# A fixed order for the first four attention tiles of a chunked-attention and two-FFN kernel

## The chip, the cores and the metric

The kernel runs on one NeuronCore of a Trainium2 chip. The metric is the device time of one execution in microseconds (us), lower is better. TensorE is called PE here, its weight loads PEld, VectorE DVE, ScalarE ACT, GpSimd POOL, SyncE SP.

## What is computed

Attention over chunks, then two feed-forward layers, all in float32 at the outputs. The inputs `q`, `k`, `v` have 4 batches, 8 heads, 768 positions and 64 columns. A chunk of 32 queries sees 8 memory keys, 16 positions to the left, its own 32 and 8 to the right, so 64 keys in all:

```python
scores = scale * q_c @ concat(mem_k, k_ctx).T      # per chunk: 32 x 64
scores = scores - max(scores)
a = exp(scores); a = a / (sum(a) + 1e-9)
out_c = a @ concat(mem_v, v_ctx)                   # 32 x 64
x = heads side by side                             # 3072 x 512
h = x @ w_in;  x = (h - tanh(h)) @ w_out           # FFN 1, 512 -> 2048 -> 512
h = x @ w_in2; y = (max(h,0) + alpha*min(h,0)) @ w_out2   # FFN 2
```

The weights arrive as 64-bit floats.

## The kernel before

**Tiles.** 128 queries are one attention tile; there are 24. FFN 1 works in six blocks of four tiles, with 16 column groups `f` of 128 hidden columns in each: `emit_h` (12 matmuls), `emit_g` (tanh and the split of the result into a high and a low part), `emit_y` (12 matmuls). FFN 2 follows with a form that needs fewer products. Every float32 operand of the FFNs is kept as a high and a low part (`fp32r`), and three products of parts make one product.

**One attention tile** takes these steps. `emit_scores` (L516): PE writes the scores `sp` to two PSUM tiles of the pool `ps_a` (two buffers); DVE takes the row maximum and the maximum is subtracted (for the first three tiles ACT copies the scores to SBUF and POOL subtracts, afterwards DVE does both), ACT takes the exponential. `emit_soft` (L557): DVE sums the row and inverts the sum, POOL multiplies. Then the 32-row blocks of the result are transposed into `ebuf`, a buffer with zeros between the blocks. For the first four tiles (`PE_T`) `emit_turn` (L581) does this on PE: products with an identity `ident` write the blocks into the PSUM tile `tp` (`ps_y`), products with a tile `zeros` write the zero blocks (L589), and ACT copies the whole `tp` to `ebuf` (L601), in two halves of four heads. Later tiles use DVE's transpose. `emit_pv` (L603): PE multiplies by the values into `pv` (`ps_h`), ACT copies it to the high part of `ring` (L616) and DVE writes the low part (L617). Block 0 of FFN 1 reads the `ring` entries of all four first tiles.

**Weights.** `split_w` (L121) converts a pair of 64-bit weight tiles of one `f`: per tile one ACT pass (L99), three DVE passes (`u` L102, L105, `s` L109), then ACT makes the high part (L115) and POOL the low part (L116). `u` lies in `ps_y` while `stage["early"]` holds, in `ps_a` afterwards.

**Order.** SP's loads of the first phase are issued in the order written: keys and queries of tiles 0 and 1 with the values of tile 0, the weight pair of `f` = 0, then the rest (`loads_to`, `loads`). All other engines are ordered by a scheduler of the compiler, from the order in which the program emits the steps: tile after tile, with the conversions of `f` = 0, 1 and 2 (`EARLY_W`) emitted at tiles 1, 4 and 5, and the scores of tile 4 before the first FFN product. In block 0 a further `f` is converted in each slot (`more_w`), and the later tiles are worked off at planned slots between the FFN products.

Of the kernel before, what the change touches and what calls it, by code (L numbers as in the profile page):

```python
# [7 lines left out]
FP32 = mybir.dt.float32  # L8
FP32R = mybir.dt.float32r
# [13 lines left out]
FIRST = 1  # L23
EARLY_W = (1, 4, 5)
PE_T = 4
ANCHOR = 'exp'
SUB_POOL = 3
# [4 lines left out]
AHEAD = 5  # L32
# [4 lines left out]
def chunk_attention_two_ffn_kernel(  # L37
# [55 lines left out]

    def to_f32(raw, dst=None):
        words = raw.bitcast(U32).rearrange("p (n two) -> p n two", two=2)
        lw, hw = words[:, :, 0], words[:, :, 1]
        pool, tag = (ps_y, "y") if stage.get("early") else (ps_a, "a")
        u = pool.tile([128, 512], U32, tag=tag, name="u")
        nc.scalar.activation(  # L99
            out=u.bitcast(FP32), in_=hw.bitcast(FP32), func=ACTF.Copy, scale=2.0 ** -112  # L100
        )
        nc.vector.tensor_scalar(  # L102
            out=u, in0=u, scalar1=3, scalar2=None, op0=ALU.logical_shift_left
        )
# [7 lines left out]
        return s.bitcast(FP32)  # L112

    def split_f32(v, hi, lo):
# [371 lines left out]
    ident = ac.tile([128, 128], FP32, name="ident")  # L486
    zeros = ac.tile([128, CH], FP32, name="zeros")
    qt, vt, kt = {}, {}, {}
# [26 lines left out]

    def emit_scores(t):  # L516
        s = t % TPS
        kn = kt.pop(t)
        sps = [ps_a.tile([128, HP, 64], FP32, tag="a", name="sp",
                         padded_shape=[128, 8, 64]) for _ in range(2)]  # L520
        for p in range(HP):
            for c in range(4):
                for j in range(2):
                    r = slice(64 * j, 64 * j + 64)
                    last["at"] = nc.tensor.matmul(  # L525
                        out=sps[j][CH * c:CH * c + CH, p, :],
                        lhsT=qt[t][r, p, CH * c:CH * c + CH],
                        rhs=kn[r, p, c // 2, CH * (c % 2):CH * (c % 2) + W + NM],
                        start=True, stop=True,
                    ).ins  # L530
        for sp in sps:
            if s == 0:
# [14 lines left out]
        else:  # L547
            for j, sp in enumerate(sps):
# [4 lines left out]
                )  # L553
        last["exp"] = nc.scalar.activation(out=sc, in_=sc, func=ACTF.Exp, scale=scale).ins
        sm[t] = sc

    def emit_soft(t):  # L557
        sc = sm.pop(t)
        sg = aw.tile([128, H, 1], FP32, tag="sg", name="sg")
# [5 lines left out]
        )  # L565
        if t < PE_T:
            return emit_turn(sc)
        et = t_p.tile([128, 512], FP32, tag="t", name="et")
# [11 lines left out]

    def emit_turn(sc):  # L581
        idn = ident.rearrange("p (a c n) -> p a c n", a=2, c=2)
        for hh in range(2):
            tp = ps_y.tile([128, 512], FP32, tag="y", name="tp")
            tp = tp[:KW].rearrange("k (a h n) -> k a h n", a=2, h=4)
            for c in range(2):
                cols = slice(CH * c, CH * c + CH)
                r = 2 * CH * (1 - c)
                nc.tensor.matmul(  # L589
                    out=tp[r:r + CH, :, :, cols], lhsT=zeros, rhs=sc[:, 4 * hh:4 * hh + 4, :],  # L590
                    start=True, stop=True,
                )
                for h in range(4):
                    for a in range(2):
# [5 lines left out]
                        )  # L600
            nc.scalar.activation(out=ebuf[:, :, 4 * hh:4 * hh + 4, :], in_=tp, func=ACTF.Copy)  # L601

    def emit_pv(t, slot):  # L603
        pv = ps_h.tile([128, 512], FP32, tag="h", name="pv")
        for p in range(HP):
            for a in range(2):
                for j in range(2):
# [3 lines left out]
                        lhsT=vt[t][:, a, D * h:D * h + D],  # L611
                        rhs=ebuf[:, a, h, :],
                        start=True, stop=True,
                    ).ins
        pvv = pv.rearrange("k (p n) -> k p n", p=HP)
        nc.scalar.activation(out=ring[0][:, slot], in_=pvv, func=ACTF.Copy)  # L616
# [49 lines left out]
    if True:  # L666
# [15 lines left out]
        n0 = blocks1[0]  # L682
        nc.gpsimd.memset(zeros, 0.0)
        nc.gpsimd.memset(ident, 0.0)
# [211 lines left out]
```

## Time and profile before

| | us |
|---|---|
| median of 3 runs (lowest, highest) | 1112.61 (1108.74, 1112.82) |
| the profiled execution, its own time | 1111.79 |
| its span, first to last instruction | 1110.0 |
| PE busy | 1082.4 (98%) |
| DVE, ACT, POOL busy | 523.6, 478.4, 426.8 |

The span is what the hardware profiler saw from the first to the last instruction; 1.8 us of the execution's own time lie around it. Busy times are sums over the span and hide that the phases have different limits: the first 50 us are attention and weight loading, the rest is the FFNs with attention tiles between their products.

### The profile page before, as it was taken

What the parts mean: (1) busy time and instruction counts of PE and PEld (TensorE: products, weight loads), DVE (VectorE), ACT (ScalarE), POOL (GpSimd) and SP (SyncE); (2) the same over time, 40 slices, a digit from 0 to 9 for tenths busy, and PEclk for the clock granted to TensorE, in tenths of its full rate; (3) what the DMA queues carried; (4) which work ended last, traced back from release to release, by engine and by line L of the source; (5) the groups of instructions that cost most, each with busy time, mean ns of one, the idle gap of its engine ahead of it and who ended that gap; (6) DMA issues with size and microseconds to landing.
All of it is one profiled execution on the core that took longest, in us unless ns stands there. A gap on an engine that the chain in (4) does not pass through costs nothing.

```text
span 1110.0 us, 17747 instructions
## 1 busy us (share of the span) xinstructions
PE 1082.4 (98%) x7056; PEld 892.5 (80%) x7056; DVE 523.6 (47%) x875; ACT 478.4 (43%) x789; POOL 426.8 (38%) x279
## 2 busy tenths in 40 slices
PE   4699999999999999999999999999999999999998
PEld 4588888888888888888888888888888888888887
DVE  3688754655646565564311466700566500566000
ACT  3566643443534444443332466520556420557300
POOL 3266633443434343344462000990002990003900
PEclk9699999999999999999999999999999999999999
DMA  9673234554454455335420663543754443751312
GB/s 275 258 265 115 77 124 171 164 147 166 143 176 176 154 162 170 125 148 189 176 67 1 232 214 110 180 164 106 234 194 152 152 161 129 246 175 39 110 43 76
DMA packets 57395, 171.04 MB, mean 154 GB/s; under 512 B 8288, under 2 KB 8544, under 8 KB 57312
## 3 DMA queue, kind: packets, MB, share of 16 engines
q1 hardware_dynamic: 53712, 163.48, 44.1%
q10 hardware_dynamic: 3600, 6.42, 1.6%
q8 instruction: 56, 0.92, 0.3%
q14 instruction: 27, 0.22, 0.1%
HBM read 134.23 MB, written 35.65 MB: 153 GB/s over the span
## 4 chain that ended last, share of the span: by engine, by line
PE 96%; DMA 2%; DVE 1%; issue 1%; POOL 0%; ACT 0%; SPq 0%; ACTq 0%; DVEq 0%; POOLq 0%
PE h L241 24%; PE y L280 24%; PE h L368 20%; PE yb L445 12%; PE y L445 12%; PE pv L609 2%; PE sp L525 2%; PE tp L596 1%; DMA qn<-in_q_dram 1%; DMA ri<-in_moe_w_in_dram 1%; DMA y1d<-ys 0%; PE tp L589 0%; DVE u L102 0%; SPq L495 0%; DVE s L109 0%
## 5 line engine op out<-in xcount | busy, mean ns | idle before, releaser
L241 PE MATMUL h<-ring,wt 128*128 128x512 f32 x1152 | 281.2, 392 | 4.0 <-ACT ring L616 2.2
L241 PEld LDWEIGHTS h<-ring,wt 128*128 128x128 f32 x1152 | 216.9, 189 | 50.7 <-ACT ring L616 2.4
L116 POOL TENSOR_TENSOR g2l<-g,g2h 128x1024 fp32r<-128x1024 f32 x48 | 121.7, 2570 | 282.1 <-ACT g2h L115 282.1
L368 PE MATMUL h<-xh,wi 128*128 128x512 f32 x672 | 209.0, 389 | 0.2 <-DVE g L385 0.2
L280 PE MATMUL y<-gh,wt 128*128 128x512 f32 x768 | 192.7, 391 | 0.0
L266 POOL TENSOR_TENSOR gl<-t,gh 128x512 fp32r<-128x512 f32 x96 | 126.7, 1320 | 155.3 <-ACT gh L265 129.2
L280 PEld LDWEIGHTS y<-gh,wt 128*128 128x128 f32 x768 | 143.2, 188 | 30.4
L368 PEld LDWEIGHTS h<-xh,wi 128*128 128x128 f32 x672 | 126.1, 188 | 27.0 <-DVE g L385 0.6
L257 DVE TENSOR_TENSOR t<-h,t 128x512 f32<-128x512 f32 x96 | 65.7, 685 | 153.6 <-ACT t L256 148.8
L256 ACT ACTIVATE t<-h 128x512 f32<-128x512 f32 x96 | 57.0, 594 | 130.2 <-PE h L241 118.8
L280 PE MATMUL y<-gl,wt 128*128 128x512 f32 x384 | 104.2, 389 | 0.0
L469 DVE COPY ys<-y 128x512 f32<-128x512 f32 x6 | 4.0, 688 | 198.6 <-PE y L445 198.6
L445 PE MATMUL y<-ring,g2h 128*128 128x512 f32 x384 | 96.3, 389 | 0.0
L445 PE MATMUL yb<-ring,g2h 128*128 128x512 f32 x384 | 96.1, 389 | 0.0
L445 PEld LDWEIGHTS y<-ring,g2h 128*128 128x128 f32 x384 | 72.1, 188 | 15.0
L445 PEld LDWEIGHTS yb<-ring,g2h 128*128 128x128 f32 x384 | 72.1, 188 | 15.0
L280 PEld LDWEIGHTS y<-gl,wt 128*128 128x128 f32 x384 | 72.0, 188 | 15.0
L265 ACT ACTIVATE gh<-t 128x512 fp32r<-128x512 f32 x96 | 60.5, 630 | 42.7 <-DVE t L257 34.9
L376 ACT ACTIVATE n<-g 128x512 f32<-128x512 f32 x72 | 45.4, 632 | 72.6 <-DVE g L385 72.2
L368 PE MATMUL h<-xl,wi 128*128 128x512 f32 x192 | 74.7, 389 | 0.0
L378 DVE SCALAR_TENSOR_TENSOR g<-g,n 128x512 f32<-128x512 f32 x72 | 62.7, 870 | 15.8 <-ACT n L377 14.5
L377 ACT ACTIVATE n<-n,alpha_neg 128x512 f32<-128x512 f32 x96 | 67.0, 717 | 1.3
(86 smaller groups left out, 1313.2 us busy)
## 6 DMA issues: line engine op xcount, KB each, us to landing
wi<-w2i SPq DMA_DIRECT2D x72, 512.0 KB, 4.4
ring<-w2o SPq DMA_DIRECT2D x48, 512.0 KB, 3.6
kn<-in_k_dram SPq DMA_DIRECT2D x24, 384.0 KB, 5.1
vn<-in_v_dram SPq DMA_DIRECT2D x24, 384.0 KB, 4.1
ri<-in_moe_w_in_dram SPq DMA_DIRECT2D x16, 512.0 KB, 8.3
ro<-in_moe_w_out_dram SPq DMA_DIRECT2D x16, 512.0 KB, 8.6
pk<-in_moe_w_in_dram SPq DMA_DIRECT2D x16, 512.0 KB, 3.7
w2i<-ws SPq DMA_DIRECT2D x16, 512.0 KB, 2.7
```

The source lines that it names most:

```text
L116: nc.gpsimd.tensor_tensor(out=lo, in0=v, in1=f32(hi), op=ALU.subtract)
L241: last["ffn"] = nc.tensor.matmul(out=h, lhsT=wi[:, a, kk, :], rhs=ring[c][:, s0:s0 + n, kk, :], start=(i == 0), stop=(i == 3 * KD - 1),).ins
L256: nc.scalar.activation(out=t, in_=h, func=ACTF.Tanh)
L257: last["dve"] = nc.vector.tensor_tensor(out=t, in0=h, in1=t, op=ALU.subtract).ins
L265: nc.scalar.activation(out=gh, in_=t, func=ACTF.Copy)
L266: nc.gpsimd.tensor_tensor(out=gl, in0=t, in1=f32(gh), op=ALU.subtract)
L280: mm = nc.tensor.matmul(out=yp[l, b][j][:, :n * 128], lhsT=wo[:, a, j * 128:(j + 1) * 128], rhs=g[c], start=first, stop=final,)
L368: nc.tensor.matmul(out=h, lhsT=w[:, a, 128 * kt:128 * kt + 128], rhs=x[c][:, kt, :], start=(first and j == 0), stop=(j == 5), skip_group_c ...
L376: nc.scalar.activation(out=n, in_=h, func=ACTF.Relu, scale=-1.0)
L377: nc.scalar.activation(out=n, in_=n, func=ACTF.Copy, scale=alpha_neg[:, f:f + 1])
L378: nc.vector.scalar_tensor_tensor(out=t, in0=h, scalar=0.0, in1=n, op0=ALU.max, op1=ALU.add)
L445: nc.tensor.matmul(out=sets[k][j], lhsT=g[a][:, k, j * 128:(j + 1) * 128], rhs=w[:, c, :], start=(f == 0 and n == 0), stop=(f == NF - 1 an ...
```

## The change

- The first four tiles are emitted in steps in one written order (`FIRST_STEPS`), and PE, ACT, DVE and POOL keep that order in this phase. A letter is a step, a digit the tile (for a, b, c the weight tile of `f` = 0): S scores, M maximum and subtraction, E exponential, N sum and multiplication, T transposes and copies, P product with the values, R `ring`; a ACT's pass over both raw weight tiles, b DVE's three passes, c the split.
- The products with `zeros` are gone. Each of the first four tiles has its own buffer `eb` in the weight pool, zeroed by a POOL memset of 96 x 1024 elements (and `ebuf` likewise for the later tiles); from `tp` only the blocks are copied, per half two copies on ACT and one on DVE.
- The loads come in another order: the first weight pair stands behind keys and queries of all four tiles and two tiles of values.
- Only `f` = 0 is converted within the fixed order. The scores of tile 4, its softmax and the conversion of `f` = 1 and 2 are emitted after it. `u` always lies in `ps_a`.

```diff
-EARLY_W = (1, 4, 5)
-PE_T = 4
+FIRST_STEPS = """
+S0 M0 S1 E0 N0 M1 E1 T0 N1 S2 M2 P0 R0 S3 E2 M3 E3 T1 N2 N3 a0 P1 b0 R1 c0 T2 b1 c1 T3 P2 R2 P3 R3
+"""
+MANUAL = ("PE", "Activation", "DVE", "Pool")
...
     def emit_turn(...):
...
-                r = 2 * CH * (1 - c)
-                nc.tensor.matmul(
-                    out=tp[r:r + CH, :, :, cols], lhsT=zeros, rhs=sc[:, 4 * hh:4 * hh + 4, :],
-                    start=True, stop=True,
-                )
...
-            nc.scalar.activation(out=ebuf[:, :, 4 * hh:4 * hh + 4, :], in_=tp, func=ACTF.Copy)
+            for c, r, n in ((0, 0, 2 * CH), (1, CH, CH), (1, 2 * CH, CH)):
+                cols = slice(CH * c, CH * c + CH)
+                o, src = eb[r:r + n, :, 4 * hh:4 * hh + 4, cols], tp[r:r + n, :, :, cols]
+                if r == 2 * CH:
+                    nc.vector.tensor_copy(out=o, in_=src)
+                else:
+                    nc.scalar.activation(out=o, in_=src, func=ACTF.Copy)
...
         with tc.manual_schedule(engines={mybir.EngineType.SP}):
-            loads_to(1)
+            for t in (0, 1):
+                load_k(t)
+                load_q(t)
+            load_v(0)
+            for t in (2, 3):
+                load_k(t)
+                load_q(t)
+            load_v(1)
             loads(1)
-            loads_to(n0 - 1)
-            load_v(n0 - 1)
+            load_v(2)
+            load_v(3)
             loads(2)
+            nk[0] = n0
             loads_to(n0)
             load_v(NS)
-        stage["early"] = True
-        for t in range(n0 + 2):
-            if t >= 2:
-                tok_c(t - 2)
-            if t <= n0:
-                emit_scores(t)
-            if t == n0:
-                loads_to(n0 + 1)
-            if 1 <= t:
-                emit_soft(t - 1)
-            for _ in range(EARLY_W.count(t)):
-                more_w()
-        stage["early"] = False
...
+        with tc.manual_schedule(engines=engines):
+            for t in range(NS):
+                ebufs[t] = w_p.tile([KW, 2, H, 2 * CH], FP32, tag="w", name="eb")
+                nc.gpsimd.memset(ebufs[t], 0.0)
+            nc.gpsimd.memset(ebuf, 0.0)
+            for w in FIRST_STEPS.split():
+                steps[w[0]](int(w[1]))
+        keep(0, 0, ws)
+        nw[0] = 1
+        loads(AHEAD)
+        behind(last["at"], emit_scores, n0)
+        loads_to(n0 + 1)
+        emit_soft(n0)
+        for _ in range(2):
+            more_w()
```

## Rows read from the trace of the kernel before

**Rows 1.** The page's first line.

```profile
span 1110.0 us, 17747 instructions
```

**Rows 2.** Busy time by stretch: length, five engines with instructions, PE clock, DMA share, GB/s.

```profile
0.00:23.30 23.30, 10.28 (x348) 9.04 (x348) 7.99 (x20) 7.79 (x15) 7.83 (x14) 1.00 0.91 272
23.30:30.10 6.80, 5.03 (x130) 4.02 (x127) 2.36 (x6) 2.79 (x5) 1.65 (x2) 0.71 1.04 292
...
49.60:64.70 15.10, 15.07 (x139) 11.72 (x143) 10.46 (x20) 9.30 (x18) 10.68 (x9) 0.87 0.32 108
64.70:95.70 31.00, 31.00 (x155) 25.58 (x145) 30.27 (x56) 21.60 (x40) 21.54 (x17) 1.00 0.60 225
95.70:137.00 41.30, 41.30 (x357) 34.05 (x356) 32.30 (x66) 25.23 (x47) 24.98 (x21) 1.00 0.33 103
137.00:1108.00 971.00, 969.09 (x5687) 799.50 (x5685) 426.75 (x681) 402.44 (x649) 356.10 (x215) 1.00 0.44 148
```

**Rows 3.** Timeline of PE: start, us, what, in brackets idle time before it.

```profile
15.72 1.32 PE L525 MATMUL sp<-kn,qn 64*32 64x64 f32 x56 [5.27 <-DVE sg L562]
...
47.04 0.80 PE L241 MATMUL h<-ring,wt 128*128 128x512 f32 x1 [2.25 <-ACT ring L616]
49.62 7.26 PE L241 MATMUL h<-ring,wt 128*128 128x512 f32 x23 [1.79 <-DVE ring L617]
...
56.82 1.15 PE L609 MATMUL pv<-ebuf,vn 96*64 96x64 f32 x32
```

**Rows 4.** Landing of the queries of tile 2, issued at 4.76 us.

```profile
L502 SPq DMA_DIRECT2D qn<-in_q_dram x1: 848/848/848, 4.8 to 4.8; - x1
...
DMA to landing us min/median/max: 10.9/10.9/10.9
```

**Rows 5.** Timeline of the other engines in the first phase.

```profile
0.73 0.12 POOL L683 MEMSET zeros<- 128x32 f32 x1 [0.29 <-POOLq L874]
0.79 0.20 POOL L684 MEMSET ident<- 128x128 f32 x1
...
7.30 1.04 POOL L546 TENSOR_TENSOR sc<-sc,mx 128x512 f32<-128x512 f32 x1 [5.93 <-DVE mx L545]
...
9.04 0.69 DVE L560 TENSOR_REDUCE sg<-sc 128x8 f32<-128x512 f32 x1 [1.82 <-ACT sc L554]
...
11.37 1.04 POOL L563 TENSOR_TENSOR sc<-sc,sg 128x512 f32<-128x512 f32 x1 [3.03 <-DVE sg L562]
...
20.68 0.37 ACT L544 ACTIVATE sc<-sp 128x256 f32<-128x256 f32 x1
```

**Rows 6.** Timeline of PE within the transposes of two tiles.

```profile
18.26 0.63 PE L589 MATMUL tp<-sc,zeros 128*32 128x256 f32 x1
...
18.68 0.63 PE L589 MATMUL tp<-sc,zeros 128*32 128x256 f32 x1
...
39.02 0.38 PE L589 MATMUL tp<-sc,zeros 128*32 128x256 f32 x1
...
39.23 0.38 PE L589 MATMUL tp<-sc,zeros 128*32 128x256 f32 x1
```

**Rows 7.** Waits of PE, 0 to 44 us: total, times, longest.

```profile
PE tp L596 <- issue: 3.9, 2, 2.2
```

**Rows 8.** DMA queues, 22 to 24 us: the queue that loads instructions.

```profile
q8 instruction: 1, 0.02, 3.5%
```

**Rows 9.** Groups of DVE instructions, 49.6 to 137 us: busy us, mean ns.

```profile
L109 DVE SCALAR_TENSOR_TENSOR s<-ri,u 128x512 uint32<-128x512 uint32 x14 | 9.4, 671 | 0.1
```

**Rows 10.** Timelines of DVE and POOL in block 0: one conversion of weights after another.

```profile
67.21 0.70 DVE L102 TENSOR_SCALAR u<-u 128x512 uint32<-128x512 uint32 x1
...
71.17 1.30 POOL L116 TENSOR_TENSOR wt<-s,wt 128x512 fp32r<-128x512 f32 x1 [3.28 <-ACT wt L115]
...
77.38 1.30 POOL L116 TENSOR_TENSOR wt<-s,wt 128x512 fp32r<-128x512 f32 x1 [1.39 <-ACT wt L115]
...
81.76 1.30 POOL L116 TENSOR_TENSOR wt<-s,wt 128x512 fp32r<-128x512 f32 x1 [0.26 <-ACT wt L115]
```

More of the change, by code (lines that the diff above doesn't have):

```diff
@@ L92, in load_raw, with words_of, to_u @@
         raws[l, i] = raw
-    def to_f32(raw, dst=None):
+    def words_of(raw):
         words = raw.bitcast(U32).rearrange("p (n two) -> p n two", two=2)
-        lw, hw = words[:, :, 0], words[:, :, 1]
+        return words[:, :, 0], words[:, :, 1]
+    def to_u(raw):
+        hw = words_of(raw)[1]
         pool, tag = (ps_y, "y") if stage.get("early") else (ps_a, "a")
@@ L101, in to_f32, with from_u @@
         )
+        return u
+    def from_u(raw, u, dst=None):
+        lw, hw = words_of(raw)
         nc.vector.tensor_scalar(
@@ L112, in to_f32 @@
         return s.bitcast(FP32)
+    def to_f32(raw, dst=None):
+        return from_u(raw, to_u(raw), dst)
     def split_f32(v, hi, lo):
@@ L514, in half, with emit_sp @@
         return x.rearrange("q (p j) n -> q p j n", j=2)[:, :, j]
-    def emit_scores(t):
-        s = t % TPS
+    spt = {}
+    ebufs = {}
+    pvt = {}
+    def emit_sp(t):
         kn = kt.pop(t)
-        sps = [ps_a.tile([128, HP, 64], FP32, tag="a", name="sp",
+        sps = spt[t] = [ps_a.tile([128, HP, 64], FP32, tag="a", name="sp",
                          padded_shape=[128, 8, 64]) for _ in range(2)]
@@ L530, in emit_scores, with emit_max @@
                     ).ins
+    def emit_max(t):
+        s = t % TPS
+        sps = spt.pop(t)
         for sp in sps:
@@ L553, in emit_scores, with emit_exp, emit_sum @@
                 )
-        last["exp"] = nc.scalar.activation(out=sc, in_=sc, func=ACTF.Exp, scale=scale).ins
         sm[t] = sc
-    def emit_soft(t):
-        sc = sm.pop(t)
+    def emit_exp(t):
+        nc.scalar.activation(out=sm[t], in_=sm[t], func=ACTF.Exp, scale=scale)
+    def emit_scores(t):
+        emit_sp(t)
+        emit_max(t)
+        emit_exp(t)
+    def emit_sum(t):
+        sc = sm[t]
         sg = aw.tile([128, H, 1], FP32, tag="sg", name="sg")
@@ L565, in emit_soft @@
         )
-        if t < PE_T:
-            return emit_turn(sc)
+    def emit_soft(t):
+        emit_sum(t)
+        sc = sm.pop(t)
         et = t_p.tile([128, 512], FP32, tag="t", name="et")
@@ L600, in emit_turn, with emit_vals @@
                         )
-            nc.scalar.activation(out=ebuf[:, :, 4 * hh:4 * hh + 4, :], in_=tp, func=ACTF.Copy)
-    def emit_pv(t, slot):
-        pv = ps_h.tile([128, 512], FP32, tag="h", name="pv")
+            for c, r, n in ((0, 0, 2 * CH), (1, CH, CH), (1, 2 * CH, CH)):
[5 more added lines that the diff above has]
+                    nc.scalar.activation(out=o, in_=src, func=ACTF.Copy)
+    def emit_pv(t, slot):
+        emit_vals(t)
+        emit_ring(t, slot)
+    def emit_vals(t):
+        eb = ebufs.pop(t, ebuf)
+        pv = pvt[t] = ps_h.tile([128, 512], FP32, tag="h", name="pv")
         for p in range(HP):
@@ L689, in chunk_attention_two_ffn_kernel, with conv_a, conv_b, conv_c @@
         with tc.manual_schedule(engines={mybir.EngineType.SP}):
-            loads_to(1)
+            for t in (0, 1):
[6 more added lines that the diff above has]
+            load_v(1)
             loads(1)
-            loads_to(n0 - 1)
-            load_v(n0 - 1)
+            load_v(2)
+            load_v(3)
             loads(2)
+            nk[0] = n0
             loads_to(n0)
             load_v(NS)
-        stage["early"] = True
-        for t in range(n0 + 2):
-            if t >= 2:
-                tok_c(t - 2)
-            if t <= n0:
-                emit_scores(t)
-            if t == n0:
-                loads_to(n0 + 1)
-            if 1 <= t:
-                emit_soft(t - 1)
-            for _ in range(EARLY_W.count(t)):
-                more_w()
-        stage["early"] = False
+        us, vs, ws = [0, 0], [0, 0], [0, 0]
+        def conv_a():
+            for i in range(2):
+                us[i] = to_u(raws[0, i])
+        def conv_b(i):
+            vs[i] = from_u(raws.pop((0, i)), us[i])
+        def conv_c(i):
+            ws[i] = w_p.tile([128, 2, 512], FP32R, tag="w", name="wt")
+            split_f32(vs[i], ws[i][:, 0], ws[i][:, 1])
+        steps = {
+            "S": emit_sp, "M": emit_max, "E": emit_exp, "N": emit_sum, "T": emit_turn,
+            "P": emit_vals, "R": lambda t: emit_ring(t, x0[0][0] + t),
+            "a": lambda i: conv_a(), "b": conv_b, "c": conv_c,
+        }
+        engines = {getattr(mybir.EngineType, e) for e in MANUAL}
+        with tc.manual_schedule(engines=engines):
[13 more added lines that the diff above has]
+            more_w()
         plan = {}
```

12 lines of the change are left out of this document (6 added, 6 removed).

## The prediction, made before the result was known

> **What bounds the kernel now.** I read the busy times by stretch first. From 49.6 us to the end of the span PE is busy without a gap: 15.07 of 15.10, 31.00 of 31.00, 41.30 of 41.30, 969.09 of 971.00 us, with the clock at its upper level after the first few us [rows 2]. All that is left to win lies in front of the first FFN products: in the first 23.3 us PE works 10.28 us, in the next 6.8 us 5.03 [rows 2]. So the time after the change is the old one, less what the first FFN product comes earlier, plus what PE waits later. That start is sharp in the timeline of PE: one product at 47.04, when the high part of `ring` is there, the others from 49.62, when DVE had written the low part, 2.6 us later [rows 3]; before that DVE had the weight conversions in its queue. Earlier, the scores of tile 2 began only at 15.72, with tile 0's transposes queued behind them [rows 3]. The row names DVE as releaser, but the queries of tile 2, issued at 4.76, landed 10.9 us later, at 15.66 [rows 4]; both raw weight tiles of `f` = 0 were ahead of them.
>
> **The change, part by part.** I follow the written order with durations from rows; each engine takes its steps in turn.
>
> *Loads.* The weight pair (1.05 MB) no longer stands ahead of tiles 2 and 3. At 272 GB/s [rows 2] that is 3.9 us; I take 13 us for the queries of tile 2 and 15.7 for tile 3 (0.66 MB more). The pair itself lands near 20. The queue stays full, so the later loads move by nothing.
>
> *Memsets.* POOL now zeroes five buffers of 1024 columns before its first subtraction. Rows show 32 columns in 0.12 and 128 in 0.20 us; a straight line gives 0.9 to 0.95 each, so POOL is done at 1.4 + 4.7 = 6.1 us. POOL's first subtraction is at 7.30 [rows 5], which covers it. Upper end: twice a 512-column operation of 1.04, 2.1 each, POOL done at 11.8; everything behind it then moves some 4 us, of which 2.2 reach the start. The line is nearer to a memset.
>
> *Zero products.* In the transposes eight narrow products and one with zeros take 18.68 - 18.26 = 0.42 us at the lower clock level (1.2 GHz) and 0.21 at the upper (2.4 GHz) [rows 6]. Eight products of 64 columns at 1.2 GHz are 0.43 by themselves: the zero product ran beside them. I count nothing for its removal; the other end is a ninth, 0.4 us per tile. A tile's transposes stay at 3.3 us (lower level) or 1.8.
>
> *Copies.* Per half two on ACT and one on DVE in place of one on ACT. The nearest row, 256 columns from PSUM, is 0.37 [rows 5]; I take 0.33 back to back on ACT, 0.38 on DVE, in sequence, since they read one PSUM tile: 1.1 us after a half's last product. Ends 0.25 and 0.6 each: -1 to +2 us at the start. They also stand in DVE's order ahead of the sums N, which wait for them.
>
> *The chain.* Tile 0's sum begins at 9.04 (0.69 and two short ones, about 1.1 together), its multiplication takes 1.04 [rows 5], now ahead of tile 1's work: done 11.3. Transposes 11.3 to 14.6, last copy 15.8. Tile 1's sum, behind that copy, to 16.8, multiplied by 17.9. Scores of tile 2 14.6 to 15.9, product of tile 0 with the values (1.15 [rows 3]) to 17.1, scores of tile 3 17.6 to 18.6, once tile 2's maximum has freed the PSUM tiles. Tile 1's transposes could begin at 18.6. Here I add a wait: within two transposes PE stood for 3.9 us in all, the longer 2.2, with nothing to wait for that the profile shows ("issue") [rows 7], and the instruction queue had a block in flight then [rows 8], with the DMA engines full. The first wait came after 348 + 348 recorded products and loads, and 130 + 127 lie between it and the next [rows 2]. In the new order some 700 are issued at the head of tile 1's transposes (64 of each for scores or transposes, 32 for the values), so I put a wait there and take 2.2: transposes 20.8 to 23.5, copies to 24.6. The sums of tiles 2 and 3 follow on DVE to 25.7 and 26.8, then `b0` (three passes, 1.8) to 28.6. PE has tile 2 from 26.8 to 30.1, tile 3 to 33.4. ACT copies tile 2 behind the split `c0` until 31.2, DVE's `b1` runs to 33.1, ACT's split to 33.7, and only then come tile 3's copies, to 35.5. Product 36.7, high part 37.3, low part 38.0. The FFN's second product starts at 38.0, not 49.62: **11.6 us earlier**.
>
> Of that wait the Trainium skill, "Runtime: NRT & Kernel Launch", section "Instruction fetch mechanics", says that the sequencer fetches the next block while the current one runs and that crossing a boundary is mostly hidden. By that page the 2.2 us fall away and the sum is 2 us better. The trace disagrees in the first phase, with the 3.9 us above, and agrees in the FFN phase, where PE runs without a gap.
>
> *What moves behind the start.* Before, tile 4's scores and softmax, all six passes of `f` = 1 and four each of `f` = 2 and 3 were done by 49.6. Now 14 passes (0.6 back to back, 0.67 alone [rows 9]) and some 2.4 us for tile 4 come after it: 10.8 us more for DVE. In block 0 it was busy 10.46 + 30.27 + 32.30 = 73.0 of 87.4 us [rows 2]; 83.8 still fits, but not at every moment. `f` = 1 is the first to be late. PE needs it after the first 12 products, 12/23 of 7.26 = 3.8 us after the start [rows 3]. DVE first does tile 4's maximum (1.4), then converts: at tile 5 the first pass began at 67.21 and the low part was done at 71.17 + 1.30, 5.3 us later [rows 10]. So 6.7 us: PE waits 2.9. The next conversions come 4.4 us apart (77.38, 81.76 [rows 10]) against 5.1 us of products per `f` (24 of 512 columns at 2.4 GHz, 0.21 each), and gain 0.7 us each; tile 5's work on DVE (an estimate from the durations above: maximum 1.4, sum 1.1, transposes and copies 2, `ring` 0.6) then falls into that, for another wait of about 1.3. **4.2 us given back.** Tile 4's scores on PE hide behind the last `ring` copies; uncovered they cost 0.9.
>
> *Sum.* 11.6 - 4.2 = 7.4: span 1110.0 [rows 1] to 1102.6, own time 1111.8 to 1104.4. The median of the runs stands 0.8 above that execution: 1105.
>
> **The rivals.**
> *Instructions arrive in time* (0.18): PE shows no wait of the kind "issue", tile 1's transposes begin at 18.6 and the start is at 36.0: 13.6 - 4.2 = 9.4, so 1103. For it: at the one place before the first wait, some 440 records in, PE stood for nothing but its own inputs. Against: the DMA engines are as full as before. It is the case that the Trainium skill's page "Runtime: NRT & Kernel Launch" states, by the section named above.
> *DVE takes it back* (0.20): all 10.8 us moved behind the start come out as PE's waits, since from 64.7 to 95.7 DVE is busy 30.27 of 31.0 [rows 2] and has no room while tile 5 and the early `f` are due. Gain 0.8: 1111.5, no change. Against: over all of block 0 it had 14 us free, most of it before 64.7 and after 95.7.
> *Slower* (0.08): the same waits, in pieces, drop PE's clock to its lower level each time. That is what the first 23 FFN products show after an idle phase: 7.26 us [rows 3] instead of 23 x 0.21 = 4.9, so 2.3 us per drop. The place is `f` = 1 to 5; with 10.8 us of waits and four drops 20 us are lost against 11.6 won: 1120. It decides once waits and drops pass 17 us. Against: a drop slows PE's demand, so DVE catches up, which limits their number.
> *Not as it says* (0.04): the fixed order waits somewhere for a buffer (`u` in `ps_a`, `pv`) long enough that the start stays near 48: 1110 to 1113.
> The forecast itself holds 0.50, 1102 to 1108.
>
> **How the numbers follow.** A measurement of this kernel can tell about 0.5% from no change, 5.6 us: faster is below 1107.0. Faster: all of the first rival and nearly all of the forecast, 0.67; same: its edge, DVE's rival and the last one, 0.25; slower 0.08. The low end 1100 is the first rival with 3 us less given back, since `emit_y` of `f` = 0 needs no new weights and could run while `f` = 1 is late; upper ends of the unknown prices (memsets 2.2, copies 2, code 1.5 more) lead from 1105 to 1110.5, into the DVE rival.
>
> **What would show it.** Right: FFN products from 36 to 40 us without the 1.8 us wait for `ring`'s low part, tile 0's transposes near 11.3, memsets of about 0.95 over before 7 us, a PE wait of 2 to 4 us before the second `f` for ACT's or POOL's weight part, PE without gaps after some 30 us more. Wrong: a start after 42 us, waits of PE in block 0 over 8 us, or a granted clock at the lower level past the first 10 us of the FFN.

## The result, and the profile after

The kernel after takes 1119.33 us (median of 5 runs, 1118.06 to 1120.49), the one before, run beside it, 1112.61 (1108.74 to 1113.20). The ratio is 1.007 with an interval of 1.0058 to 1.0081: 0.7% slower, where 1105.0 was forecast and 1100 to 1110.5 was the range. The profiled execution took 1118.06 us, 1.8 of them around its span, as before [rows 1]:

```profile
span 1116.3 us, 17699 instructions
```

The timeline of PE in the kernel after tells most of it (start, duration, what; in brackets the idle time before it and what ended it):

```profile
11.47 3.63 PE L619 MATMUL tp<-ident,sc 128*32 128x64 f32 x64 [2.09 <-POOL sc L587]
15.03 1.06 PE L538 MATMUL sp<-kn,qn 64*32 64x64 f32 x64
...
18.04 1.14 PE L538 MATMUL sp<-kn,qn 64*32 64x64 f32 x60 [0.87 <-DVE mx L562]
23.03 0.42 PE L538 MATMUL sp<-kn,qn 64*32 64x64 f32 x4 [3.85 <-issue]
23.38 3.09 PE L619 MATMUL tp<-ident,sc 128*32 128x64 f32 x64
29.69 1.98 PE L643 MATMUL pv<-eb,vn 96*64 96x64 f32 x32 [3.21 <-DVE eb L628]
32.83 5.26 PE L619 MATMUL tp<-ident,sc 128*32 128x64 f32 x128 [1.16 <-POOL sc L587]
...
41.92 1.84 PE L643 MATMUL pv<-eb,vn 96*64 96x64 f32 x32 [2.75 <-DVE eb L628]
...
44.80 3.70 PE L252 MATMUL h<-ring,wt 128*128 128x512 f32 x12
54.58 5.75 PE L252 MATMUL h<-ring,wt 128*128 128x512 f32 x12 [6.08 <-ACT wt L126]
60.41 1.15 PE L643 MATMUL pv<-ebuf,vn 96*64 96x64 f32 x32
61.49 2.12 PE L291 MATMUL y<-gh,wt 128*128 128x512 f32 x8
```

Three things are to be seen. First, up to 18 us all runs as forecast: the transposes of tile 0 at 11.47 and the scores of tile 2 right behind them at 15.03, no longer waiting for their queries (15.72 before [rows 3]). Second, between 19 and 42 us PE idles in places that the forecast lacked or priced lower: 3.85 us for instructions, in front of the last four products of tile 3's scores, then 3.21 and 2.75 for copies. Third, the FFN starts at 44.80, and behind its first twelve products PE stands for 6.08 us; tile 4's product, at 56.82 before [rows 3], comes at 60.41, later than it was.

A checkpoint makes the sum. I take the second FFN product: its input `ring`'s low part is written at 44.43 + 0.69 = 45.12 (the DVE rows below), against 49.62 before, so **4.5 us were won** at the start where 11.6 were forecast. From there to the end of the span it is 1116.3 - 45.1 = 1071.2 us against 1110.0 - 49.6 = 1060.4: **10.8 us were given back** where 4.2 were forecast. 10.8 - 4.5 = 6.3, the difference of the spans.

What holds the last four products is instructions. In the stretches of 2 us below (length, PE, PEld, DVE, ACT, POOL busy, granted clock, DMA share, GB/s) the DMA engines are full and from 20 to 22 us PE does nothing; the clock is at 0.59 afterwards, and again 0.66 (between its two levels of 1.2 and 2.4 GHz) where the second `h` follows its wait:

```profile
12.00:14.00 2.00, 2.00 (x45) 2.00 (x41) 0.00 (x0) 1.18 (x3) 0.41 (x1) 1.00 1.03 271
...
16.00:18.00 2.00, 1.17 (x39) 1.01 (x32) 1.87 (x6) 1.25 (x3) 0.33 (x1) 1.00 1.05 258
...
20.00:22.00 2.00, 0.00 (x0) 0.00 (x0) 0.00 (x0) 0.38 (x1) 0.00 (x0) 1.00 1.02 308
22.00:24.00 2.00, 0.97 (x16) 0.81 (x18) 0.42 (x1) 0.00 (x0) 0.00 (x0) 0.59 1.02 402
...
50.00:60.00 10.00, 5.27 (x12) 3.64 (x12) 8.03 (x17) 6.02 (x13) 4.86 (x4) 0.66 0.38 151
```

In that wait the queue that loads instructions has a block in flight (DMA queues of the kernel after, 20 to 22 us: packets, MB, share), as in [rows 8]:

```profile
q8 instruction: 1, 0.02, 3.8%
```

Such waits are not new: the kernel before stood 1.77 and 2.16 us for instructions, 3.9 in all [rows 7]. There DVE and ACT were busy for 1.9 and 1.8 of 3.8 us meanwhile (23.4 to 25.1 and 30.5 to 32.6 us); in the fixed order they stand still with PE, as the row of 20 to 22 us shows.

The timeline of DVE in the kernel after, around tile 3's maximum and behind the start:

```profile
26.59 0.42 DVE L567 TENSOR_TENSOR sc<-sp,mx 128x256 f32<-128x256 f32 x1 [2.61 <-PE tp L619]
...
30.46 0.69 DVE L584 TENSOR_REDUCE sg<-sc 128x8 f32<-128x512 f32 x1
...
44.43 0.69 DVE L653 TENSOR_TENSOR ring<-pv,ring 128x512 fp32r<-128x512 f32 x1 [0.89 <-ACT ring L652]
...
51.43 0.71 DVE L596 STREAM_TRANSPOSE et<-sc 128x512 f32<-128x512 f32 x1 [1.25 <-POOL sc L587]
52.07 0.65 DVE L117 SCALAR_TENSOR_TENSOR s<-ri,u 128x512 uint32<-128x512 uint32 x1
52.64 0.68 DVE L117 SCALAR_TENSOR_TENSOR s<-ro,u 128x512 uint32<-128x512 uint32 x1
```

And of ACT:

```profile
27.90 0.63 ACT L574 ACTIVATE sc<-sc 128x512 f32<-128x512 f32 x1 [7.52 <-DVE sc L567]
28.44 1.54 ACT L630 ACTIVATE eb<-tp 64x256 f32<-64x256 f32 x4
...
52.18 1.70 ACT L603 ACTIVATE ebuf<-et 32x256 f32<-32x256 f32 x4 [4.28 <-DVE et L596]
53.90 0.63 ACT L126 ACTIVATE wt<-s 128x512 fp32r<-128x512 f32 x1
```

At 26.59 DVE's subtraction for tile 3 waits for PE's transposes of tile 1. The pool `g_p` has two buffers for `sc`, so tile 3's `sc` gets the buffer of tile 1, which PE reads until then. Behind it in the written order stand ACT's exponential of tile 3 (27.90), the copies of tile 1 behind that (28.44, 2 us after the end of the transposes at 26.47), and DVE's two sums (30.46), though tile 2's exponential was over at 20.4. Behind the start, tile 4's softmax stands ahead of `f` = 1: the transpose, which waits 1.25 us for POOL, ahead of the last pass on DVE, and four copies ahead of the weights' high part on ACT, which PE waits for until 54.53. Later PE waits four times for DVE, as the row of its waits after 62 us says (total, times, longest); in the kernel before a single wait of 0.2 us was left there:

```profile
PE h L252 <- DVE t L268: 2.0, 4, 1.0
```

The memsets are as forecast (timeline of POOL):

```profile
1.26 3.63 POOL L762 MEMSET eb<- 96x1024 f32 x4
4.83 0.95 POOL L763 MEMSET ebuf<- 96x1024 f32 x1
```

My theory after this: (1) the instruction wait, stretched by full DMA engines, (2) the shared buffer, (3) the order of tile 4 and `f` = 1 behind the start. The rival to (1) is that the wait belongs to that place whatever the loads do; to (3), that DVE simply has too much to do before PE can go on, in any order.

### The profile page after: what moved, and what is told of

Read it like the earlier page. It is cut to its first block, busy times and chain, and to the rows that moved or that the text cites. A ratio compares the mean times of both kernels' runs of the same rounds, so it can differ in the third digit from the quotient of the medians.

```text
span 1116.3 us, 17699 instructions
## 1 busy us (share of the span) xinstructions
PE 1083.2 (97%) x7024; PEld 892.5 (80%) x7024; DVE 528.7 (47%) x883; ACT 479.4 (43%) x797; POOL 433.1 (39%) x283
## 4 chain that ended last, share of the span: by engine, by line
PE 90%; DVE 4%; DMA 2%; ACT 2%; issue 1%; POOL 1%; ACTq 0%; SPq 0%; DVEq 0%; POOLq 0%
PE y L291 21%; PE h L379 20%; PE h L252 20%; PE yb L456 12%; PE y L456 12%; PE pv L643 2%; PE sp L538 1%; DMA pk<-in_moe_w_in_dram 1%; DMA y1d<-ys 1%; DVE u L110 1%; DVE u L113 1%; PE tp L619 1%; DMA w2o<-pk 1%; DVE sg L584 0%; DVE s L117 0%
```

## The experiments

Start is the first FFN product, y0 the first product of `emit_y`, both in us and like the span from the profiled execution of each kernel; ratios are to the kernel before, run on the same chip, with their 95% interval.

| kernel | start | y0 | span | median us (runs) | ratio |
|---|---|---|---|---|---|
| before | 47.04 | 57.90 | 1110.0 | 1112.61 (5) | |
| after | 44.80 | 61.49 | 1116.3 | 1119.33 (5) | 1.007 (1.0058 to 1.0081) |
| own_buffer | 43.19 | 60.35 | 1115.9 | 1116.52 (5) | 1.004 (1.0027 to 1.0053) |
| weights_first | 45.19 | 60.72 | 1115.9 | 1117.17 (6) | 1.0041 (1.0029 to 1.0054) |
| buffer_and_weights | 43.49 | 59.48 | 1113.7 | 1115.48 (7) | 1.003 (1.0019 to 1.0041) |
| after_loads_held | 40.14 | 57.29 | 1111.1 | 1113.06 (10) | 1.0011 (1.0002 to 1.0021) |
| loads_held | 36.78 | 52.04 | 1105.9 | 1108.61 (6) | 0.9972 (0.9959 to 0.9984) |
| reordered | 38.61 | 54.32 | 1107.6 | 1110.57 (10) | 0.9991 (0.9981 to 1.0000) |

One reading helps with all of these: from y0 to the end of the span it is 1052.1 us before, 1054.8 after, and 1053.3 to 1055.6 in the others. So of the 6.3 us between the spans of before and after, 3.6 lie ahead of y0 and 2.7 behind it, and the versions of the table differ by up to 9.5 us ahead of y0 and by up to 3.5 behind it. From start to y0 it is 10.9 us before, but 15.3 to 17.2 in every version of the table with the fixed order.

**The shared buffer** (own_buffer, of the kernel after):

```diff
-        if t <= NS:
+        if t == NS - 1:
+            sc = w_p.tile([128, H, 64], FP32, tag="w", name="sc")
+        elif t <= NS:
             sc = g_p.tile([128, H, 64], FP32, tag="gh", name="sc")
```

> The changed kernel, with the scores of tile 3 in a buffer of their own; nothing else differs. Theory (buffer): the subtraction of tile 3 on DVE stood 2.6 us and its exponential held ACT's copies of tile 1 until 28.4, because tile 3's scores reuse the buffer that tile 1's transposes still read. Then the subtraction starts near 24.0 instead of 26.6, tile 1's copies on ACT near 25.0 instead of 28.4, and the first FFN product 2 to 3.5 us earlier, at 41.3 to 42.8 instead of 44.8; the total falls by 1.5 to 3.5 us, to about 1116.5. Rival (instructions): the chain hangs on PE's wait of 3.85 us before the last products of tile 3's scores alone, and the first FFN product stays within 0.5 us of 44.8.

Measured: 1116.52, 2.8 us less than after. Timeline of PE in own_buffer:

```profile
23.94 0.42 PE L538 MATMUL sp<-kn,qn 64*32 64x64 f32 x4 [4.88 <-issue]
...
43.19 4.09 PE L252 MATMUL h<-ring,wt 128*128 128x512 f32 x12
```

The start is 1.6 us earlier although the instruction wait was 1.0 longer here. The subtraction of tile 3 begins at 24.92, with its scores, not at the end of the transposes. The wait behind the start stays, 6.15 before 53.43. So the buffer was a real cause, of about 2.8 us by the medians; the intervals of the two ratios don't touch, though the two profiled spans differ by 0.4 us only.

**`f` = 1 ahead of tile 4** (weights_first, of the kernel after: `more_w` twice, then `emit_soft(n0)`; buffer_and_weights: with own_buffer's edit as well):

```diff
-        emit_soft(n0)
         for _ in range(2):
             more_w()
+        emit_soft(n0)
```

> The changed kernel, with the conversions of f = 1 and 2 emitted ahead of tile 4's softmax instead of behind it. Theory (place in the order): the second h waited 6.1 us because DVE's last pass over the weights of f = 1 stood in DVE's order behind tile 4's transposes, which wait for POOL, and ACT's split behind four copies of tile 4. Then that wait falls to 2 to 3 us and the total by 3 to 5 us, to about 1115. Rival (DVE is full): the 10.8 us of work moved behind the start have to come out somewhere; the wait before the second h shrinks but reappears before tile 4's product or the next h, and the total stays within 1.5 us of 1119.3.

> Both edits together. If both theories hold they add: 1119.3 - 2.5 - 4 = 1113, no slower than the kernel before (1112.6). If the start is won only to be lost behind it (DVE is full), the first FFN product is near 42 and the total no better than that of the better single edit.

Measured: 1117.17, 2.2 less than after; both edits 1115.48, 3.9 less. Timeline of PE in weights_first:

```profile
51.23 0.73 PE L252 MATMUL h<-ring,wt 128*128 128x512 f32 x2 [1.70 <-ACT wt L126]
52.58 2.60 PE L252 MATMUL h<-ring,wt 128*128 128x512 f32 x10 [0.62 <-POOL wt L127]
...
58.76 2.03 PE L643 MATMUL pv<-ebuf,vn 96*64 96x64 f32 x32 [3.58 <-ACT ebuf L603]
60.72 3.78 PE L291 MATMUL y<-gh,wt 128*128 128x512 f32 x8
```

The wait of 6.08 becomes 1.70 + 0.62, and 3.58 come back one step later, where PE wants tile 4's `ebuf`: 5.9 in all, so the wait only changed its place: PE needs both the weights of `f` = 1 and tile 4's `ebuf` before y0. The later waits on `t` fall from 2.0 to 0.3, but the first eight products of y take 3.78 us here against 2.12, and the profiled spans differ by 0.4 us only, so where the 2.2 us of the medians come from is not shown.

**The zero products** (zeros_back: the matmul with `zeros` as `lhsT` put back into `emit_turn` of the kernel after, with its memset).

> The changed kernel with the 16 products with zeros put back into the transposes, their blocks still not copied. Forecast of the prediction: they run beside the narrow products and cost nothing, total within 1 us of 1119.3. Rival: each takes an own slot of a ninth of the group, 0.4 us per tile at the lower clock, so 0.8 to 1.6 us on the chain of tiles 1 to 3, and 64 more PE instructions move the place of the instruction wait from the end of tile 3's scores to some 10 products earlier.

Measured: 1118.02 (1117.83 to 1119.12), ratio 1.0054 (1.0039 to 1.0069), not distinguishable from after. Eight narrow products with the zero product among them follow each other every 0.42 us (24.25, 24.68, 25.11), as in [rows 6]. Their removal is worth nothing that these runs can tell, as forecast. The instruction wait changed its length, 4.88, with 12 products left behind it instead of 4. The place follows a count: the trace has 8 more products ahead of it here, and the wait comes 8 products earlier in the work, after 348 recorded products in both kernels.

**The loads** (loads_held, of buffer_and_weights; after_loads_held: the same edit of the kernel after). A step `L0` behind `R0` holds everything behind `load_v(1)`: DVE writes one column of the first weight tile, and SP, now in the fixed order too, issues that load and the later ones only then. That load then overwrites the column.

```diff
-... P0 R0 S3 E2 ...
-MANUAL = ("PE", "Activation", "DVE", "Pool")
+... P0 R0 L0 S3 E2 ...
+MANUAL = ("PE", "Activation", "DVE", "Pool", "SP")
...
         raw = w_p.tile([128, 512], U64, tag="w", name=name)
+        if stage.pop("hold", False):
+            nc.vector.memset(raw.bitcast(FP32)[:, 0:1], 0.0)
...
             load_v(1)
+        def held():
+            stage["hold"] = True
             loads(1)
```

> The kernel buffer_and_weights, with all loads behind the values of tile 1 held back until DVE has passed the low part of tile 0 (near 18.9 us), by a one-column write of DVE into the next load's buffer. Theory (instruction blocks behind data): PE's wait of 5.2 us before the last products of tile 3's scores is its next block of instructions on its way among saturated data loads; with the DMA engines idle from about 15 to 19 us the block arrives in time, the wait falls under 1 us, tile 1's transposes begin near 19.5 instead of 24.7, and the first FFN product comes 2 to 4 us earlier than in buffer_and_weights (43.5), since the first weights then land near 22 instead of 18 and hold back b0. Rival (the wait is a property of the place): a wait of 3 us or more stays before the last products of tile 3's scores.

> The changed kernel with the held loads alone (same hold as in loads_held; tile 3's scores share a buffer with tile 1's again, and tile 4's softmax stands ahead of the weights of f = 1 again). Theory: the wait for instructions is the largest single cause of the late start. The wait goes, tile 1's transposes begin near 18.7, and since they then end near 20.7 the shared buffer costs little: first FFN product near 38 instead of 44.8; the 6 us wait before the second h stays. Total near 1119.3 - 6.5 = 1113, the time of the kernel before. Rival: the shared buffer keeps the start above 40, total above 1115.

Measured: 1108.61, 6.9 less than buffer_and_weights; 1113.06, 6.3 less than after. Busy time by stretch in loads_held:

```profile
16.00:18.00 2.00, 1.03 (x33) 0.73 (x39) 1.90 (x6) 0.71 (x2) 0.81 (x1) 1.00 0.03 8
18.00:20.00 2.00, 2.00 (x111) 1.91 (x109) 1.55 (x5) 0.63 (x1) 1.23 (x2) 1.00 0.35 68
```

Its instruction queue from 16 to 18 us:

```profile
q8 instruction: 1, 0.02, 3.0%
```

Timeline of PE in buffer_and_weights:

```profile
24.35 0.42 PE L538 MATMUL sp<-kn,qn 64*32 64x64 f32 x4 [5.17 <-issue]
24.71 3.63 PE L621 MATMUL tp<-ident,sc 128*32 128x64 f32 x64
```

And in loads_held:

```profile
17.55 1.20 PE L540 MATMUL sp<-kn,qn 64*32 64x64 f32 x64 [0.93 <-DVE mx L566]
18.68 1.98 PE L623 MATMUL tp<-ident,sc 128*32 128x64 f32 x64
...
37.48 2.79 PE L254 MATMUL h<-ring,wt 128*128 128x512 f32 x11 [0.20 <-DVE ring L657]
43.04 0.73 PE L254 MATMUL h<-ring,wt 128*128 128x512 f32 x2 [2.77 <-ACT wt L128]
...
50.59 1.52 PE L647 MATMUL pv<-ebuf,vn 96*64 96x64 f32 x32 [2.04 <-ACT ebuf L607]
52.04 3.44 PE L293 MATMUL y<-gh,wt 128*128 128x512 f32 x8
```

With the DMA engines at 0.03 before the place where PE stood, the block of instructions is in flight at 16 to 18 us, not at 20 to 22, and the wait is gone: all 64 products of tile 3's scores run on end, the transposes of tile 1 begin at 18.68 (the prediction's first rival said 18.6) and take 1.98 us. In buffer_and_weights they take 3.63 behind a wait of 5.17 us, at a granted clock of 0.50 (24 to 28 us), so part of what the hold wins is PE's clock. PE's products and their order are the same in both kernels, so the length of the wait does not belong to the place: the block comes late beside the loads. The hold is no free gift: the weights land later, and ACT waits 1.98 us for them at 24.61. The start came 6.7 us earlier than in buffer_and_weights, more than the 2 to 4 that were expected, and the median fell by as much. In after_loads_held the total is what its theory said, but the start, 40.14, is where its rival had it: PE still waits 3.21 us for the copies of tile 1, as in the kernel after, whose shared buffer it has.

**The parts of the change by themselves**, in the kernel before: only the new order of loads (before_new_loads), and only the own buffers, memsets and block copies without zero products (before_new_transposes), both in the compiler's order.

> The kernel before, with the new order of the loads alone. Theory: the loads are worth little alone, because the scheduler's order of the engines was made without knowing when a load lands: tile 2's scores begin near 13 instead of 15.7, but the conversions of f = 0 stand in DVE's and ACT's queues ahead and wait for weights that land 3 to 4 us later; the first FFN product within 2 us of before, total within 3 us of 1112. Rival: the loads were the whole gain of the start, 3 us or more.

> The kernel before, with the new transposes alone: zeroed buffers, no products with zeros, only the blocks copied, engines ordered by the scheduler as before. Theory: nothing, within 3 us of 1112: the products ran beside others, the memsets end before POOL's first subtraction, and three copies of 1.1 us take the place of one of 0.6. Rival: PE's lower load or the own buffers (four in place of one) let the tiles overlap and bring the start 3 us or more forward.

Measured: 1110.97, ratio 0.9990 (0.9975 to 1.0004), and 1114.77, ratio 1.0028 (1.0018 to 1.0038). In before_new_loads tile 2's scores begin at 11.44 instead of 15.72, yet the second FFN product only 0.6 us earlier (48.99): PE waits 1.79 us for `ring`'s low part from DVE there, as in [rows 3]. In before_new_transposes tile 4's product comes at 57.84 against 56.82 [rows 3]; PE waits 7.0 us in all for DVE's copies to `eb`. Neither part wins alone. If the parts add up, which no run shows, -0.1% and +0.3% leave most of the 0.7% to what wasn't tried by itself: the fixed order, with `f` = 1 and 2 and tile 4 behind it.

**Another order** (reordered, of buffer_and_weights: the conversion of `f` = 0 ahead of tile 3's maximum, `u` in `ps_y`, an own `sc` for tile 2 as well):

```diff
-S3 E2 M3 E3 T1 N2 N3 a0 P1 b0 R1 c0 T2 b1 c1 T3 P2 R2 P3 R3
+S3 E2 N2 a0 b0 c0 b1 c1 M3 E3 T1 N3 T2 P1 R1 T3 P2 R2 P3 R3
```

> The kernel buffer_and_weights, with another written order: S0 M0 S1 E0 N0 M1 E1 T0 N1 S2 M2 P0 R0 S3 E2 N2 a0 b0 c0 b1 c1 M3 E3 T1 N3 T2 P1 R1 T3 P2 R2 P3 R3, u of f = 0 in the other PSUM pool and tile 2's scores too in a buffer of their own. Theory (order): while PE waits for instructions (19 to 24 us) DVE and ACT can do tile 2's sum and the whole conversion of f = 0, which stood in between the later tiles' copies; then T2 follows T1 at once, and the first FFN product is near 37.5 instead of 43.5, the total near 1109.5, better than both kernels. Rival (DVE is full behind the start): the first FFN product comes as early, but the second h waits as much longer, and the total stays within 2 us of 1115.5.

Measured: 1110.57, ratio 0.9991 (0.9981 to 1.0000). PE's wait for instructions is still 3.9 us, but DVE converts beside it, and the start comes 4.9 us earlier than in buffer_and_weights, which is what the total gained. So most of what that wait costs is the written order standing still behind it. The order, `u`'s pool and tile 2's own buffer changed together here; what each is worth alone was not tried.

**Behind the start.** Two attempts to use the earlier start. held_p4_later, of loads_held, plans tile 4's product two slots later. held_f1_first, of that, brings N2 and T1 forward in the order and converts `f` = 1 in it as well, with `u` in `ps_y` and own `sc` buffers for tiles 2 and 3:

```diff
-                todo.append((release(n0), 10 * t - 9, tok_c, n0))
+                todo.append((2, 10 * t - 9, tok_c, n0))
...
-L0 S3 E2 M3 E3 T1 N2 N3 a0 P1 b0 R1 c0 T2 b1 c1 T3 P2 R2 P3 R3
+L0 S3 E2 M3 N2 T1 E3 N3 P1 R1 a0 b0 T2 c0 T3 P2 R2 P3 R3 a2 b2 c2 a1 b1 c1 a3 b3 c3
```

> The kernel loads_held with tile 4's product with the values planned two slots later, behind the first y. Theory (place in the order): PE's 2.0 us wait for tile 4's copies before that product goes, and with it part of the stretch at the lower clock level: total 1108.6 - 2 to 3 = about 1106. Rival (DVE is full): the next product waits instead, total within 1 us of 1108.6.

> The kernel held_p4_later with another written order that ends with the conversion of f = 1: S0 M0 S1 E0 N0 M1 E1 T0 N1 S2 M2 P0 R0 L0 S3 E2 M3 N2 T1 E3 N3 P1 R1 a0 b0 T2 c0 T3 P2 R2 P3 R3 a2 b2 c2 a1 b1 c1 a3 b3 c3 (0, 1 the pair of f = 0, 2, 3 that of f = 1, L0 the hold). Theory: the start is set by the written order and by when the weights land, the waits behind it by what stands ahead of f = 1 on DVE: first FFN product near 32 to 34 instead of 37, wait before the second h at most 2 us, total near 1103, faster than the kernel before by 0.7%. Rival (DVE is full): with 73 us of DVE work due in block 0 before and some 6 us more here, PE waits for weights later in block 0 (f = 3 to 8), and the total stays at 1106 or above.

Measured: 1108.20 (10 runs), ratio 0.9978 (0.9966 to 0.9990), and 1108.04 (10 runs), ratio 0.9969 (0.9959 to 0.9979): both like loads_held. In held_p4_later the wait before tile 4's product is gone, and PE waits 2.47 us for DVE before the next `h` instead. Timeline of PE in held_f1_first:

```profile
35.21 7.87 PE L254 MATMUL h<-ring,wt 128*128 128x512 f32 x24
50.16 4.53 PE L254 MATMUL h<-ring,wt 128*128 128x512 f32 x12 [7.08 <-DVE t L270]
```

Timeline of DVE in held_f1_first ahead of that:

```profile
48.23 0.70 DVE L600 STREAM_TRANSPOSE et<-sc 128x512 f32<-128x512 f32 x1
48.85 0.67 DVE L112 TENSOR_SCALAR u<-u 128x512 uint32<-128x512 uint32 x1
49.43 0.68 DVE L270 TENSOR_TENSOR t<-h,t 128x512 f32<-128x512 f32 x1
```

This start, 35.2, is earlier than all above and runs 24 products without a wait, and then PE stands 7.08 us for DVE's pass on the first `h`, which stands behind conversions and tile 4's transpose. Is that order, or amount? g0_in_order puts that `h` and its split (`H0`, `G0`) into the written order, which ends `R3 H0 a2 b2 c2 a1 b1 c1 G0 a3 b3 c3`:

> held_f1_first with the first FFN group's products (H) and its tanh and split (G) put into the fixed order, G behind the conversion of f = 1's input weights and ahead of its output weights; nothing is left out. If the wait of 7.1 us there is the order on DVE (its pass for t stands behind ten passes and a transpose), it falls to 3 to 4 us, the wait for f = 2's weights takes its place, and the median goes from 1108.0 to 1103.5 to 1106. If DVE has too much to do before PE can go on, whichever comes first, the wait moves whole and the median stays at 1107 to 1109.

Measured: 1112.31 (11 runs), ratio 1.0013 (1.0002 to 1.0025), 4.3 us slower than held_f1_first and outside both expectations. Waits of PE in g0_in_order up to 140 us (total, times, longest):

```profile
PE h L254 <- ACT wt L128: 3.5, 1, 3.5
PE pv L647 <- DVE t L270: 1.9, 1, 1.9
...
PE y L293 <- ACT gh L278: 1.3, 2, 0.9
PE y L293 <- DVE s L119: 0.9, 1, 0.9
```

Its busy time by stretch, 50 to 60 us:

```profile
50.00:60.00 10.00, 7.50 (x47) 5.26 (x46) 9.81 (x18) 6.92 (x14) 5.46 (x5) 0.67 0.79 314
```

PE now begins `emit_y` at 41.69, but the 7.1 us come back as 3.5 + 1.9 + 1.3 + 0.9, with the clock at 0.67 between them; DVE is busy 9.81 of 10 us, and the product that follows y of `f` = 1 comes at 63.71, against 63.10 in held_f1_first. By tile 5's product with the values it is 2.7 us behind (95.85 against 93.11). A better place for one wait won nothing, and y0 at 41.69, the earliest of all, went with a longer total.

The last three runs take work away instead: the second of DVE's three passes is left out for the ten weight tiles of `f` = 1 to 5, some 6.7 us, in the kernel after, in loads_held and in held_f1_first (the signs of these weights are lost).

```diff
-        nc.vector.scalar_tensor_tensor(
-            out=u, in0=hw, scalar=0x80000000, in1=u, op0=ALU.bitwise_and, op1=ALU.bitwise_or
-        )
+        if not stage.get("cut"):
+            nc.vector.scalar_tensor_tensor(
+                out=u, in0=hw, scalar=0x80000000, in1=u, op0=ALU.bitwise_and, op1=ALU.bitwise_or
+            )
```

> The kernel after without the second of the three DVE passes (the sign bit) of the ten weight tiles of f = 1 to 5: 10 x 0.67 = 6.7 us less for DVE behind the start, so the signs of these weights are lost. If what is given back behind the start is DVE's occupancy, most of it returns: median 1119.3 to 1113 to 1115, the 6.1 us wait before the second f 1.3 to 2 us shorter, no later waits on t. If it is the written order (tile 4's softmax ahead of f = 1) only the two passes ahead of f = 1's parts count: 1117 to 1118.5. If it is PE's clock or the loads: no change, 1119.

> loads_held without the same ten passes (the signs of the weights of f = 1 to 5 are lost). DVE's occupancy theory: the remaining waits (2.8, 2.0) shrink by 1 to 3 us: 1108.6 to 1104 to 1107. Rival (clock, order on ACT, transfers): 1108 to 1109.

> held_f1_first without the same passes (four of the ten now in the fixed order, the signs of the weights of f = 1 to 5 are lost). DVE's occupancy theory: the wait of 7.1 us for g of the first f shrinks by 3 to 6 us, and the total with it: 1108.0 to 1102 to 1105, so the earlier start is at last worth something. Rival: the wait stays or comes back elsewhere, 1107 to 1108.5.

Measured: 1116.35 (5 runs; 3.0 less than after), 1108.60 (11 runs; no change), 1104.94 (5 runs; 3.1 less than held_f1_first). The ratios are 1.0045 (1.0029 to 1.0061), 0.9972 (0.9962 to 0.9983) and 0.9949 (0.9932 to 0.9965); the first and the third just overlap with those of the kernels that keep the passes, so the 3 us are at the edge of what these runs tell. The first lies outside all three ranges expected. In the kernel after, the wait for `f` = 1 falls from 6.1 to 5.3 and the later waits on `t` from 2.0 to 0.4. In held_f1_first the wait falls from 7.1 to 4.7. In loads_held the wait for the weights falls from 2.8 to 1.0, but the one for tile 4's copies grows from 2.0 to 3.8; and in that execution the start came 1.9 us later, at 38.68, in code that the edit doesn't touch. So the amount of DVE's work is probably part of what is given back, some 3 us in two kernels of three for 6.7 taken away; the rest is not settled between ACT's copies, the latencies from engine to engine and PE's clock.

## Why the prediction was wrong

*What held.* That the change is decided before the FFN runs dense, and how the sum is made. Tile 2's scores no longer wait (15.03; forecast 14.6). The memsets took 0.95 each and were over at 5.78 (forecast 6.1). The zero products were worth nothing. The copies cost about what was said: 1.54 / 4 = 0.38 on ACT and 0.42 on DVE, against 0.33 and 0.38. The chain up to tile 3's scores was right within 0.5 us.

*The instruction wait: mechanism right, term mis-sized.* The prediction put 2.2 us at the head of tile 1's transposes, by the count of 348 products in [rows 2]; the wait came after 348 products indeed, four before the end of tile 3's scores, and took 3.85, and in other kernels with almost the same code 3.9 to 5.2. Transposes of tile 1 began at 23.38, not 20.8: 2.6 us. The case of the Trainium skill, "Runtime: NRT & Kernel Launch", section "Instruction fetch mechanics", that crossing a boundary is mostly hidden, fails here beside full DMA engines and holds in loads_held, where they are at 0.03.

*The step that failed: "transposes 20.8 to 23.5, copies to 24.6".* The prediction gave no time to tile 3's maximum and exponential, which the written order puts ahead of tile 1's copies. It had a rival for a wait on a buffer, but looked for it in PSUM (`u` in `ps_a`, `pv`); the buffer was `sc` in SBUF. From the first of tile 1's transposes to its last copy it forecast 3.8 us; 7.0 passed in the kernel after and 4.9 in own_buffer, so the shared buffer is 2.1 of the 3.2. The copies of tile 1 ended at 30.4, 5.8 late with the instruction wait, and all that the written order has behind them moved along: tiles 2 and 3 were transposed from 32.83, not from 26.8. From there to the start 1 us more was lost: 45.1 in place of 38.0, 7.1 us in all.

*The other step that failed: "4.2 us given back".* Measured 10.8. The prediction counted 6.7 us until `f` = 1 is ready; it took 9.4 (45.12 to 54.53), since tile 4's sum, transpose and copies, which the prediction placed after it, came ahead. So the wait was 6.08, not 2.9. But the order is not all of it: with `f` = 1 first (weights_first) this wait was 2.3, and PE then stood 3.58 us for tile 4's copies ahead of y0. That second wait the prediction put at nothing: it priced `f` = 1 alone, where PE needs both. The second `h` ran with the clock at 0.66: the 23 products behind the checkpoint and the wait among them end at 60.41, 15.3 us after it, against 7.2 before, so 2.0 of the 8.1 us are not the wait. Another 2.0 are waits on `t` later, for which 1.3 was allowed (with 4.4 us from one conversion to the next; the pair of rows ahead of it in [rows 10], 71.17 and 77.38, is 6.2 apart). 0.7 stays unassigned. The forecast left PE's clock out, though [rows 3] gave its price for one of the rivals.

Together 7.1 + 6.6 = 13.7 us, which is 6.3 + 7.4, from the forecast's span to the measured one.

*The rivals.* "Slower", at a chance of 0.08, gave 1120 and named waits with drops of the clock. It is nearest in time and not in mechanism: it asked for 17 us behind the start, there were 10.8, and the start's own 11.6 were 4.5. "DVE takes it back" named the very 10.8 us that were given back, but that is luck: it counted them as waits, and the waits make 8.1 of them; taking 6.7 us of DVE's work away won some 3 us in two kernels and none in the third. The signs that the text gave for "wrong", a start after 42 us and over 8 us of waits in block 0, both came (6.08 + 2.0). Two failures at once, one ahead of the start and one behind it, had no chance of their own: the range was made from single failures, and here they added up.

*One reading to mend.* The prediction called 0.42 us for eight narrow products the lower clock level. The granted clock says 1.00 in that stretch, before [rows 2] and after (the row of 12 to 14 us), while tile 0's transposes took 3.63; in loads_held the same number of products took 1.98 at 18.68, also at 1.00. The same eight products with one of zeros take 0.42 us at 29.43 in the kernel before too, where the granted clock is 0.50 (28 to 30 us). So the duration is that of the lower level, but in the first 15 us the granted clock doesn't show it.

**A faster version.** loads_held and held_f1_first beat both kernels: ratios 0.9972 (0.9959 to 0.9984) and 0.9969 (0.9959 to 0.9979) to the kernel before, 0.3%. Of an FFN start some 12 to 14 us earlier (37.5 and about 35.7 for the second product, against 49.62) 3 us reach the end.

## What to carry to other kernels

Before an order is written out by hand, list for each step the buffer it writes and who still reads it: in a fixed order one shared buffer, or one late block of instructions, holds every engine. In a phase with full DMA engines leave a gap in the loads ahead of the place where PE needs its next instructions. Work that is taken from in front of a start has to be priced up to every point where PE needs it, not up to the first: here the weights of `f` = 1 and tile 4's copies were both due before y0. And an early product is no measure of the total: the first FFN product came 10 us earlier in loads_held and nearly 12 in held_f1_first for 3 us in all, and g0_in_order brought y0 itself forward and lost.

## What the runs showed of the hardware that was not expected

- The wait for a block of instructions has a fixed place. In every kernel above in which PE stood 3.8 us or more for nothing but instructions, 348 products and 348 weight loads are recorded ahead of the wait, whatever these products are, and so it is with the first wait of the kernel before; its second comes 127 of each later, and waits of 1.5 to 1.7 us in reordered, held_f1_first and g0_in_order come after 602 products, twice 127 behind 348.
- Its length is not a constant: at that place 3.85, 4.14, 4.88, 4.88, 4.85, 5.17 and 3.88 us (after, weights_first, own_buffer, zeros_back, after_fewer_passes, buffer_and_weights, reordered) with the loads running, 0.89 or 0.52 (after_loads_held, held_fewer_passes) and none (loads_held) with the loads held.
- The same 64 transposing products took 3.63 us at 11.47 in the kernel after and 1.98 at 18.68 in loads_held, both in stretches with a granted clock of 1.00; in buffer_and_weights 3.63 again at 24.71, with a granted clock of 0.50.
- After a wait of 6 us the next twelve products of 512 columns took 5.75 us, against 2.88 where PE had not stood still (76.31 in the kernel after); the granted clock is 0.50 from 54 to 58 us, and 1.00 at 76.31.
